# Fused top-k attention and two gated MLPs on one core: where the sign word of the float64 weights is made

## The chip, the cores and the metric

The kernel runs as one program on one core of one Trainium2 chip. The core has five engines with instruction queues of their own that run in order: TensorE (PE in the rows; PEld is its weight load), VectorE (DVE), ScalarE (ACT), GpSimd (POOL) and SyncE (SP), which here only issues DMAs. The metric is the device time of one execution in microseconds (us), lower is better; the median of several executions is compared.

## The reference

q, k and v are float32, 4 batches x 8 heads x 576 tokens x 64. The weights of the two MLPs are not cast: they arrive as float64 in their raw bytes, so the kernel has to turn pairs of 32-bit words into float32 by itself.

```python
scores = scale * np.matmul(q, k.transpose(0, 1, 3, 2))
kth = np.partition(scores, -32, axis=-1)[..., -32:-31]
scores = np.where(scores >= kth, scores, -1e9)
attn = np.exp(scores - np.max(scores, axis=-1, keepdims=True))
attn = attn / (np.sum(attn, axis=-1, keepdims=True) + 1e-09)
x = np.matmul(attn, v)            # to 2304 tokens x 512
g = x @ w_gate                    # 512 x 1536
x = (g / (1 + np.exp(-g)) * (x @ w_val)) @ w_out
h = x @ w_in                      # 512 x 2048
out = (h * np.cos(h)) @ w_out2
```

## The kernel before

**Stages.** The 18 tiles of 128 tokens are cut into ten chunks, two of one tile and eight of two. Each chunk runs through attention for 4 pairs of heads; a unit is one tile and one head, 144 in all. For a unit TensorE makes the scores (L609), ScalarE copies them out (L614), VectorE finds the 32 largest by four rounds of MAX8 (L637) with three MATCH_REPLACE8 between (L640), GpSimd makes two bounds from them (L651, L655), ScalarE makes the exponentials (L668, L679), TensorE transposes them (L701), ScalarE empties PSUM (L706), TensorE multiplies with v (L739, L742). The first MLP follows chunk by chunk behind attention: plain matmuls for the first two chunks (L977, L1043), and for the other eight matmuls with weights and activations split into two float32r parts (L888, L1100). The second MLP (L1313, L1377) comes when all chunks are done and takes the last third of the time.

**Conversion.** One piece of weights is 128 x 512 float64, that is two interleaved int32 planes, the high word `h` and the low word `l`. `convert` issues, for each piece: `cv_high` and `cv_low` on ScalarE (L213, L216), which scale the words in place; one instruction that makes the sign word `y`; `cv_join` on VectorE (L227, called the join below), which shifts `h` and ORs the sign into it; and `cv_add` on GpSimd (L230), an integer add of both words. There are 68 pieces. In 48 of them (24 of the first MLP's gate and value weights, 24 of the second MLP's weights, converted early during attention) the sign is made by `cv_sign` on GpSimd (L224) into an SBUF tile `c0` or `c1`. In the other 20 (12 of the first MLP's output weights, 8 of the second MLP's) it is made by `cv_minus` on ScalarE (L220) into a PSUM tile `y` or `cy`. The 24 pieces of the first MLP use the tiles `c0` and `c1` in turn, so a sign of one piece can be written only when the join two pieces earlier has read its tile; the 24 early pieces of the second MLP use `c1` for the sign and `c0` for the sum.

**Order.** Nothing is scheduled at run time. A planner (`Plan`) runs over all these steps when the program is built: each step yields an engine, a cost in us, a due time and its readiness, and the planner emits, for each engine, the ready step with the earliest due time. Its costs are only numbers in the code; they set the order in which the instructions stand in the engines' queues. On the chip each queue then runs in that order, and an instruction whose input is not there holds up everything behind it on its engine. So a change of a cost, or of a step's engine, rearranges all five queues a little.

Of the kernel before, what the change touches and what calls it, by code (L numbers as in the profile page):

```python
# [9 lines left out]
F32 = mybir.dt.float32  # L10
F32R = mybir.dt.float32r
I32 = mybir.dt.int32
# [3 lines left out]
OP = mybir.AluOpType  # L16
# [6 lines left out]
DM = H * D  # L23
# [133 lines left out]
def topk_attention_moe_moe(ctx: ExitStack, tc: tile.TileContext, qT, kT, vP, w1, wo1, w2, out):  # L157
    nc = tc.nc
# [17 lines left out]
    pools = {}  # L176
# [31 lines left out]
    def due_unit(u):  # L208
        return u * PACE


    def cv_high(h):
        nc.scalar.activation(h.bitcast(F32), h.bitcast(F32), AF.Copy, scale=2.0 ** -112)  # L213

    def cv_low(l):
        nc.scalar.activation(l.bitcast(U32), l.bitcast(U32), AF.Copy, scale=2.0 ** -29)  # L216

    def cv_minus(h, y):

        nc.scalar.activation(y, h.bitcast(F32), AF.Prelu, bias=0.0, scale=2.0 ** 40, alpha=2.0 ** 127)  # L220

    def cv_sign(h, y):

        nc.gpsimd.tensor_scalar(y, h.bitcast(F32), 0.0, -2.0 ** 31, op0=OP.is_lt, op1=OP.mult)  # L224

    def cv_join(h, y):
        nc.vector.scalar_tensor_tensor(h, h, 3, y, op0=OP.logical_shift_left, op1=OP.bitwise_or)  # L227

    def cv_add(h, l, x):
        nc.gpsimd.tensor_tensor(x, h, l, op=OP.add)  # L230

    r_pre, r_wo, r_sign, r_cy2 = Ring(6), Ring(2), Ring(1), Ring(1)
    r_c = [Ring(1) for _ in range(2)]
# [3 lines left out]
    def words(raw):  # L237
        w = raw.rearrange("p (n t) -> p n t", t=2)
        return w[:, :, 1], w[:, :, 0]

    def conv_tile(i):
        return pools["conv"].tile([128, DM], I32, tag=f"c{i}", name=f"c{i}")

    def convert(raw, due, gates, sign, on_act=False, into=None):

        h, l = words(raw)
        yield "ACT", 0.54, lambda: cv_high(h), due, True
        yield "ACT", 0.54, lambda: cv_low(l), due, False
        for gate in gates:
            yield gate  # L250
        st = {}

        def minus():
            st["y"] = sign()
            (cv_minus if on_act else cv_sign)(h, st["y"])

        yield "ACT" if on_act else "POOL", 0.54 if on_act else 0.72, minus, due, not on_act
        joined = yield "DVE", 0.63, lambda: cv_join(h, st["y"]), due, True
        t = yield "POOL", 1.25, lambda: cv_add(h, l, into() if into else l), due, True
        return joined, t  # L260

    W1X, W1, WO = {}, {}, {}
# [6 lines left out]
    def slot(i):  # L269
        return f"w{i - 1}" if i else "wx"  # L270
# [43 lines left out]
    def wo_turn(c, f):  # L314
        return ev_wol.setdefault(c * NF1 + f, Event())
# [5 lines left out]
    def wo_index(c, f):  # L321
        return c * NF1 + f
# [4 lines left out]
    def wo0_free(f, t):  # L327
        r_c[f % 2].free(W1_C + f // 2, t, plan)

    def wo0_proc(f):  # L330

        due = WO_FIRST + WO_STEP * f
        yield r_wo.gate(f)
        st = {}
        if f:
            yield wo_turn(0, f - 1)

        def load():
            st["raw"] = moe.tile([128, DM], I64, tag="wo", name="wo", bufs=r_wo.n)
            nc.sync.dma_start(st["raw"], wo1[f])  # L340

        t = yield "DMA", 2.1, load, due - 6.0, True
        wo_turn(0, f).set(t - plan.LAT["DMA"], plan)
        yield r_c[f % 2].gate(W1_C + f // 2)

        def into():
            WO[f] = conv_tile(f % 2)
            return WO[f]

        joined, t = yield from convert(st["raw"].bitcast(I32), due, [r_sign.gate(f)], lambda: yt[1].bitcast(I32),  # L350
                                       True, into)
        r_sign.free(f, joined, plan)
        r_wo.free(f, t, plan)
        WO[f] = WO[f].bitcast(F32)
        ev_wo[0, f].set(t, plan)
        t = yield "DMA", 1.1, lambda: nc.sync.dma_start(wo32[f], WO[f]), due, True
        wo_whole[f].set(t, plan)
        wo0_free(f, t)
# [6 lines left out]
    def w2_early_proc(i):  # L365
        f, half = divmod(i, 2)
        due = due_unit(46 + 3.8 * i)
        yield ev_w1s[2 * NF1 - 1]
        yield r_raw.gate(i)
        k = W1_C + WO_C + i  # L370
        cs = slice(half * DM, half * DM + DM)
        st = {}

        def load():
            st["raw"] = wpool.tile([128, DM], I64, tag=f"w{2 * NF1 - 1}", name="w2_raw")
            nc.sync.dma_start(st["raw"], w2[f, :, cs])

        yield "DMA", 2.1, load, due - 8.0, True
        yield r_c[0].gate(k)

        def into():
            st["x"] = conv_tile(0)
            return st["x"]

        joined, t = yield from convert(st["raw"].bitcast(I32), due, [r_c[1].gate(k)], lambda: conv_tile(1), False, into)
        r_c[1].free(k, joined, plan)
        r_raw.free(i, t, plan)
        t = yield "DMA", 1.1, lambda: nc.sync.dma_start(w2d[f, :, cs], st["x"].bitcast(F32)), due, True
        r_c[0].free(k, t, plan)
        w2_stored[f].set(t, plan)  # L390
# [801 lines left out]
    def w2_proc(i):  # L1192
        f, half = divmod(i, 2)
        due = T2 - 60.0 + 2.0 * i
        yield ev_pb
        st = {}
        if f < NS2:
            yield w2_stored[f]
            yield r_cvx2.gate(i)

            def load():
                st["x"] = pools["pbc"].tile([128, 512], I32, tag="cvx", name="cvx", bufs=r_cvx2.n)
                nc.sync.dma_start(st["x"].bitcast(F32), w2d[f, :, half * 512:half * 512 + 512])

            yield "DMA", 1.05, load, due, True
        else:
            pc = pools["pbc"]
            n = i - 2 * NS2
            yield r_raw2.gate(n)

            def load():
                st["raw"] = pc.tile([128, DM], I64, tag="w2s", name="w2s", bufs=r_raw2.n)
                nc.sync.dma_start(st["raw"], w2[f, :, half * DM:half * DM + DM])

            yield "DMA", 2.1, load, due, True
            yield r_cvx2.gate(i)

            def into():
                st["x"] = pc.tile([128, DM], I32, tag="cvx", name="cvx", bufs=r_cvx2.n)
                return st["x"]  # L1220

            joined, t = yield from convert(
                st["raw"].bitcast(I32), due, [r_cy2.gate(n)],
                lambda: pools["psB"].tile([128, DM], I32, tag="cy", name="cy", bufs=r_cy2.n), True, into)
            r_cy2.free(n, joined, plan)
            r_raw2.free(n, t, plan)
        if f < NF1:
            yield ev_gemm[NCH - 1, f]
        elif f < NB:
            yield ev_pbx  # L1230
        else:
            yield r_wo.gate(wo_index(NCH, half))
        x = st["x"].bitcast(F32)

        def hi():
            if f < NF1:
                pool, tag, bufs = wpool, slot(i), 1
            elif i == 2 * NB - 1:
                pool, tag, bufs = wpool, f"w{2 * NF1 - 1}", 1
            elif f < NB:  # L1240
                pool, tag, bufs = pools["pbx"], f"w{f}{half}", 1
            else:
                pool, tag, bufs = moe, "wo", r_wo.n
            st["w"] = W2[f, half] = pool.tile([128, 2, DM], F32R, tag=tag, name=f"w2_{f}", bufs=bufs)
            nc.scalar.activation(st["w"][:, 0], x, AF.Copy)  # L1245

        yield "ACT", 0.52, hi, due, True
        eng, name, cost = (nc.vector, "DVE", 0.75) if i % 3 == 2 else (nc.gpsimd, "POOL", 1.25)
        t = yield name, cost, lambda: eng.tensor_sub(st["w"][:, 1], x, st["w"][:, 0]), due, True  # L1249
        r_cvx2.free(i, t, plan)  # L1250
        ev_w2[f].set(t, plan)
# [158 lines left out]
    for f in range(NF1):  # L1410
        plan.start(wo0_proc(f))
    for i in range(2 * NS2):
        plan.start(w2_early_proc(i))
# [21 lines left out]
    for i in range(2 * NF2):  # L1435
        plan.start(w2_proc(i))
# [46 lines left out]
```

## Time and profile before

| what | value |
|---|---|
| median of 3 runs | 1317.35 us (1317.04 to 1320.25) |
| the profiled execution, its own time | 1314.26 us |
| its span, first to last instruction | 1312.5 us |
| mean granted TensorE clock | 0.975 of full |
| busy: PE, DVE | 1206.4 us, 1019.3 us |
| busy: ACT, POOL | 941.3 us, 723.6 us |

Times within the span are counted from its first instruction. Busy time of an engine is the time in which one of its instructions ran. "Idle before" and "waits" name the instruction that waited, and after the arrow what ended its wait last. In a row, `w_raw` is a piece of raw weights, `c` a sign tile, `wo` a piece of output weights with its sign in `y`, `sc` and `s` scores, `b` the bounds, `e` the exponentials, `tp` and `pt` their transposes.

### The profile page before, as it was taken

To read this page: it belongs to the slowest core of one execution; us is meant where nothing else is said; L and a number is where in the kernel's file an instruction comes from. 1 tells how busy PE (TensorE), PEld (TensorE's weight loads), DVE (VectorE), ACT (ScalarE), POOL (GpSimd) and SP (SyncE) were. 2 spreads that over 40 slices of the span, in tenths; PEclk is the share of its full clock that TensorE was granted. 3 is DMA by queue.
4 is the path that set the end of the run, shared out by engine and by line. 5 is a ranking of instruction groups with operands and counts; after the bars stand their busy time and mean duration, and the time that the engine had idled before them with its cause. 6 is when DMAs were issued, how large, how long until landed. Compare 5 with 4: busy or idle time off the path is not lost. (4 is left out here: it accounts for less than half of the span.)

```text
span 1312.5 us, 24509 instructions
## 1 busy us (share of the span) xinstructions
PE 1206.4 (92%) x8544; PEld 1096.7 (84%) x8544; DVE 1019.3 (78%) x2024; ACT 941.3 (72%) x2116; POOL 723.6 (55%) x1087
## 2 busy tenths in 40 slices
PE   2557897899999999999999999998999999999998
PEld 2346575799998899999999999997999999999997
DVE  5888999999999999999999998146655555555554
ACT  5666899888888888888788887447654555555554
POOL 6998578898878887887777765555210000000000
PEclk9768899999999999999999999998999999999999
DMA  6452445455555555546454532584110100000000
GB/s 209 136 189 85 140 158 155 149 158 190 176 160 176 174 173 160 176 147 194 146 164 141 169 115 82 175 283 163 35 43 7 35 14 24 26 8 30 1 25 24
DMA packets 83100, 157.97 MB, mean 120 GB/s; under 512 B 16672, under 2 KB 35104, under 8 KB 82976
## 3 DMA queue, kind: packets, MB, share of 16 engines
q1 hardware_dynamic: 82976, 156.41, 37.6%
q8 instruction: 67, 1.10, 0.3%
q14 instruction: 57, 0.47, 0.1%
HBM read 131.20 MB, written 25.17 MB: 119 GB/s over the span
## 5 line engine op out<-in xcount | busy, mean ns | idle before, releaser
L637 DVE MAX8 m<-w 128x8 f32<-128x576 f32 x432 | 310.4, 744 | 0.8
L888 PE MATMUL gv<-xh,w 128*128 128x256 f32 x1344 | 286.9, 292 | 3.3 <-ACT hg L856 3.3
L888 PEld LDWEIGHTS gv<-xh,w 128*128 128x128 f32 x1344 | 224.4, 190 | 8.4 <-ACT hg L856 4.5
L1313 PE MATMUL h<-x2h,w 128*128 128x384 f32 x768 | 214.1, 340 | 5.5 <-DVE g L1347 5.5
L640 DVE MATCH_REPLACE8 w<-m,w 128x576 f32<-128x576 f32 x288 | 212.7, 740 | 0.0
L1377 PE MATMUL o<-w,gh 128*128 128x512 f32 x576 | 196.4, 396 | 0.0
L888 PE MATMUL gv<-xl,w 128*128 128x256 f32 x672 | 189.7, 282 | 0.0
L1280 POOL TENSOR_TENSOR x2l<-x,x2h 128x384 fp32r<-128x384 f32 x24 | 25.5, 1061 | 252.2 <-ACT x2h L1269 252.2
L1100 PE MATMUL y<-gh,wo 128*128 128x256 f32 x768 | 158.8, 288 | 0.3 <-DMA wo<-wo 0.3
L609 PE MATMUL sc<-K,q 128*128 128x288 f32 (+1 forms) x640 | 127.2, 327 | 30.5 <-DVE K L478 11.4
L1313 PEld LDWEIGHTS h<-x2h,w 128*128 128x128 f32 x768 | 141.6, 189 | 10.5 <-DVE g L1347 6.5
L701 PE MATMUL tp<-ident,e 128*128 128x128 f32 x648 | 113.9, 287 | 33.1 <-ACT pt L706 27.3
L1347 DVE TENSOR_TENSOR g<-r,h 128x384 f32<-128x384 f32 x96 | 53.1, 554 | 115.4 <-ACT r L1342 115.4
L706 ACT ACTIVATE pt<-tp 128x512 f32<-128x512 f32 (+1 forms) x216 | 106.8, 494 | 34.2 <-PE tp L701 32.3
L1313 PE MATMUL h<-x2l,w 128*128 128x384 f32 x384 | 130.1, 339 | 0.0
L1100 PEld LDWEIGHTS y<-gh,wo 128*128 128x128 f32 x768 | 126.2, 190 | 4.3 <-issue 3.6
L609 PEld LDWEIGHTS sc<-K,q 128*128 128x128 f32 (+1 forms) x640 | 98.3, 199 | 37.3 <-DVE K L478 8.8
L888 PEld LDWEIGHTS gv<-xl,w 128*128 128x128 f32 x672 | 128.0, 190 | 0.0
L1340 ACT ACTIVATE r<-r 128x384 f32<-128x384 f32 x96 | 50.3, 525 | 108.3 <-DVE r L1337 108.3
L1377 PEld LDWEIGHTS o<-w,gh 128*128 128x128 f32 x576 | 108.7, 189 | 21.2
L668 ACT ACTIVATE e<-s,b 128x576 f32<-128x576 f32 x144 | 112.9, 784 | 14.2 <-POOL b L651 13.8
L701 PEld LDWEIGHTS tp<-ident,e 128*128 128x128 f32 x648 | 80.7, 146 | 49.9 <-ACT pt L706 38.4
(122 smaller groups left out, 2998.5 us busy)
## 6 DMA issues: line engine op xcount, KB each, us to landing
wo<-wo SPq DMA_DIRECT2D x96, 512.0 KB, 3.7
w_raw<-in_w SPq DMA_DIRECT2D x48, 512.0 KB, 5.1
V<-in_vP SPq DMA_DIRECT2D x52, 256.0 KB, 3.1
kx<-in_kT SPq DMA_DIRECT2D x64, 144.0 KB, 3.0
qx<-in_qT SPq DMA_DIRECT2D x64, 128.0 KB, 3.0
wo<-in_wo SPq DMA_DIRECT2D x12, 512.0 KB, 3.8
wo<-wo SPq DMA_DIRECT2D x24, 256.0 KB, 2.9
w2d<-c SPq DMA_DIRECT2D x24, 256.0 KB, 2.8
```

Of the source, the lines that this page charges most:

```text
L609: nc.tensor.matmul(sc[:r1, s, :HALF], q[:, a, t * 128:t * 128 + r1], k[:, s * HALF:s * HALF + HALF], start=a == 0, stop=a == 1)
L637: nc.vector.max(out=st["m"][:, 8 * i:8 * i + 8], in_=st["w"] if i else st["s"])
L640: nc.vector.match_replace(out=st["w"], in_to_replace=st["m"][:, 8 * i:8 * i + 8], in_values=st["w"] if i else st["s"], imm_value=LOWEST)
L668: nc.scalar.activation(st["e"], st["s"], AF.Prelu, bias=st["b"][:, 1:2], scale=SCALE, alpha=STEEP)
L701: nc.tensor.transpose(st["ps"][:, j - j0], e[:, j * 128:j * 128 + 128], ident)
L706: lambda: nc.scalar.activation(ptT[c, p, t][:, j0:j1], st["ps"][:, :j1 - j0], AF.Copy),
L888: nc.tensor.matmul(gv[g], W1[f, kk // 2][:, a, g, kk % 2], m[:, kk], start=kk == 0 and i == 0, stop=kk == KT - 1 and i == 2)
L1100: nc.tensor.matmul(y1p[d // 2][:, d % 2], w[:, a, d * 128:d * 128 + 128], m, start=f == 0 and i == 0 and d % 2 == 0, stop=f == NF1 - 1 and ...
L1313: nc.tensor.matmul(st["h"], w[:, a, kk * 128:kk * 128 + 128], m[:, kk], start=kk == 0 and n == 0, stop=kk == KT - 1 and n == 2)
L1340: yield "ACT", 0.41, lambda: nc.scalar.activation(r, r, AF.Abs), due, True
L1347: nc.vector.tensor_mul(st["g"], r, h)
L1377: nc.tensor.matmul(o[t], a[:, cs], W2[f, 1][:, m], start=f == 0 and n == 0, stop=f == NF2 - 1 and n == 2)
```

## The change

`cv_sign` is removed, and all 68 pieces make their sign by `cv_minus`, a leaky ramp on ScalarE: positive inputs are scaled by 2^40, negative ones by 2^40 x 2^127, and the conversion to int32 on output saturates at the lowest integer, which is the sign word. For the 48 pieces it writes the same SBUF tiles `c0` and `c1` as before. In the planner the step is charged 0.54 us to ScalarE instead of 0.72 us to GpSimd and stands directly behind `cv_low`, and the add on GpSimd is charged 1.04 us instead of 1.25.

```diff
--- before.py
+++ after.py
@@ -219,10 +219,6 @@
 
         nc.scalar.activation(y, h.bitcast(F32), AF.Prelu, bias=0.0, scale=2.0 ** 40, alpha=2.0 ** 127)
 
-    def cv_sign(h, y):
-
-        nc.gpsimd.tensor_scalar(y, h.bitcast(F32), 0.0, -2.0 ** 31, op0=OP.is_lt, op1=OP.mult)
-
     def cv_join(h, y):
         nc.vector.scalar_tensor_tensor(h, h, 3, y, op0=OP.logical_shift_left, op1=OP.bitwise_or)
 
@@ -241,7 +237,7 @@
     def conv_tile(i):
         return pools["conv"].tile([128, DM], I32, tag=f"c{i}", name=f"c{i}")
 
-    def convert(raw, due, gates, sign, on_act=False, into=None):
+    def convert(raw, due, gates, sign, into=None):
 
         h, l = words(raw)
         yield "ACT", 0.54, lambda: cv_high(h), due, True
@@ -252,11 +248,11 @@
 
         def minus():
             st["y"] = sign()
-            (cv_minus if on_act else cv_sign)(h, st["y"])
-
-        yield "ACT" if on_act else "POOL", 0.54 if on_act else 0.72, minus, due, not on_act
+            cv_minus(h, st["y"])
+
+        yield "ACT", 0.54, minus, due, False
         joined = yield "DVE", 0.63, lambda: cv_join(h, st["y"]), due, True
-        t = yield "POOL", 1.25, lambda: cv_add(h, l, into() if into else l), due, True
+        t = yield "POOL", 1.04, lambda: cv_add(h, l, into() if into else l), due, True
         return joined, t
 
     W1X, W1, WO = {}, {}, {}
@@ -348,7 +344,7 @@
             return WO[f]
 
         joined, t = yield from convert(st["raw"].bitcast(I32), due, [r_sign.gate(f)], lambda: yt[1].bitcast(I32),
-                                       True, into)
+                                       into)
         r_sign.free(f, joined, plan)
         r_wo.free(f, t, plan)
         WO[f] = WO[f].bitcast(F32)
@@ -382,7 +378,7 @@
             st["x"] = conv_tile(0)
             return st["x"]
 
-        joined, t = yield from convert(st["raw"].bitcast(I32), due, [r_c[1].gate(k)], lambda: conv_tile(1), False, into)
+        joined, t = yield from convert(st["raw"].bitcast(I32), due, [r_c[1].gate(k)], lambda: conv_tile(1), into)
         r_c[1].free(k, joined, plan)
         r_raw.free(i, t, plan)
         t = yield "DMA", 1.1, lambda: nc.sync.dma_start(w2d[f, :, cs], st["x"].bitcast(F32)), due, True
@@ -1221,7 +1217,7 @@
 
             joined, t = yield from convert(
                 st["raw"].bitcast(I32), due, [r_cy2.gate(n)],
-                lambda: pools["psB"].tile([128, DM], I32, tag="cy", name="cy", bufs=r_cy2.n), True, into)
+                lambda: pools["psB"].tile([128, DM], I32, tag="cy", name="cy", bufs=r_cy2.n), into)
             r_cy2.free(n, joined, plan)
             r_raw2.free(n, t, plan)
         if f < NF1:
```

The line numbers of the changed kernel are 4 lower from `cv_join` on (L223 is the join, L226 the add). The rows below are from the instruction queues of the two programs; the letters behind an underscore are buffer numbers.

VectorE, around the first joins, before:

```order
L637 MAX m<-w 128x8 x2
L640 MATCH_REPLACE w<-m,w 128x576
L637 MAX m<-s 128x8
L637 MAX m<-w 128x8
L227 SCALAR_TENSOR_TENSOR w_raw<-w_raw,c_229 128x512
L227 SCALAR_TENSOR_TENSOR w_raw<-w_raw,c_239 128x512
L640 MATCH_REPLACE w<-m,s 128x576
```

and the same place in the changed kernel:

```order
L633 MAX m<-w 128x8 x2
L636 MATCH_REPLACE w<-m,w 128x576
L223 SCALAR_TENSOR_TENSOR w_raw<-w_raw,c_221 128x512
L633 MAX m<-w 128x8
L223 SCALAR_TENSOR_TENSOR w_raw<-w_raw,c_237 128x512
L633 MAX m<-s 128x8 x2
L636 MATCH_REPLACE w<-m,s 128x576
```

The joins stand two instructions or one earlier among the searches and no longer back to back.

ScalarE at the same time, before (L213 and L216 are the two passes over `h` and `l`):

```order
L213 ACTIVATE w_raw<-w_raw 128x512
L473 ACTIVATE K<-kx 128x576
L216 ACTIVATE w_raw<-w_raw 128x512
L213 ACTIVATE w_raw<-w_raw 128x512
L216 ACTIVATE w_raw<-w_raw 128x512
L213 ACTIVATE w_raw<-w_raw 128x512
L216 ACTIVATE w_raw<-w_raw 128x512
L668 ACTIVATE e<-s,b_236 128x576
```

and in the changed kernel:

```order
L213 ACTIVATE w_raw<-w_raw 128x512
L469 ACTIVATE K<-kx 128x576
L216 ACTIVATE w_raw<-w_raw 128x512
L220 ACTIVATE c_221<-w_raw 128x512
L213 ACTIVATE w_raw<-w_raw 128x512
L216 ACTIVATE w_raw<-w_raw 128x512
L220 ACTIVATE c_237<-w_raw 128x512
L664 ACTIVATE e<-s,b_230 128x576
L213 ACTIVATE w_raw<-w_raw 128x512
L216 ACTIVATE w_raw<-w_raw 128x512
L523 ACTIVATE q<-qx 128x128
L220 ACTIVATE c_259<-w_raw 128x512
```

The sign instruction (L220) follows the two passes of its piece, and the third piece is begun after the first exponential and not ahead of it.

GpSimd at the same time, before:

```order
L478 TENSOR_TENSOR K<-kx,K 64x576
L224 TENSOR_SCALAR c_229<-w_raw 128x512
L651 TENSOR_TENSOR b_236<-m,cst 128x2
L224 TENSOR_SCALAR c_239<-w_raw 128x512
L655 TENSOR_TENSOR b_236<-b_236 128x1
L651 TENSOR_TENSOR b_244<-m,cst 128x2
L655 TENSOR_TENSOR b_244<-b_244 128x1
L230 TENSOR_TENSOR w_raw<-w_raw 128x512 x2
```

and in the changed kernel:

```order
L474 TENSOR_TENSOR K<-kx,K 64x576
L647 TENSOR_TENSOR b_230<-m,cst 128x2
L651 TENSOR_TENSOR b_230<-b_230 128x1
L226 TENSOR_TENSOR w_raw<-w_raw 128x512
L647 TENSOR_TENSOR b_245<-m,cst 128x2
L226 TENSOR_TENSOR w_raw<-w_raw 128x512
L651 TENSOR_TENSOR b_245<-b_245 128x1
```

The two sign instructions (L224) that stood ahead of and between the small instructions of the bounds `b` are gone from this queue.

## Rows read from the trace of the kernel before

**Rows 1.** Busy time of each engine by stretch (us); (x) counts instructions

```profile
core 0: us, PE busy (x) PEld busy (x) DVE busy (x) ACT busy (x) POOL busy (x), PEclk, DMA share, GB/s
...
15.00:110.00 95.00, 49.94 (x241) 38.53 (x242) 78.95 (x152) 66.07 (x143) 88.96 (x95) 0.80 0.53 173
...
160.00:200.00 40.00, 37.82 (x222) 29.07 (x220) 39.90 (x82) 39.47 (x90) 31.91 (x52) 1.00 0.47 154
200.00:250.00 50.00, 40.33 (x247) 28.01 (x246) 50.00 (x110) 44.38 (x100) 40.46 (x56) 0.93 0.46 134
250.00:800.00 550.00, 537.75 (x4827) 513.82 (x4826) 534.91 (x1110) 459.89 (x1112) 437.68 (x727) 1.00 0.52 163
...
905.00:1312.00 407.00, 401.61 (x1992) 362.11 (x1992) 218.16 (x387) 226.17 (x439) 31.96 (x28) 0.99 0.08 26
```

**Rows 2.** Waits from 15 to 110 us: us in total, times, longest

```profile
DVE w_raw L227 <- POOL c L224: 15.9, 16, 2.3
...
ACT e L668 <- POOL b L651: 12.9, 8, 3.5
ACT s L614 <- PE sc L609: 5.4, 5, 2.9
ACT rs L787 <- PE tp L781: 5.3, 4, 1.9
...
PE tp L701 <- ACT pt L706: 16.4, 7, 5.0
```

**Rows 3.** GpSimd groups by line, 15 to 110 us: busy us, mean ns, idle before

```profile
L224 POOL TENSOR_SCALAR c<-w_raw 128x512 int32<-128x512 f32 x21 | 42.9, 2045 | 0.1
L230 POOL TENSOR_TENSOR w_raw<-w_raw 128x512 int32<-128x512 int32 x21 | 22.1, 1059 | 2.4 <-DVE w_raw L227 1.4 <-ACT e L679 0.9
```

**Rows 4.** The join on VectorE by line, 15 to 110 us

```profile
L227 DVE SCALAR_TENSOR_TENSOR w_raw<-w_raw,c 128x512 int32<-128x512 int32 x21 | 19.2, 912 | 16.1 <-POOL c L224 15.9
```

**Rows 5.** The join in the whole span, by tile: ns least, median, most

```profile
L227 DVE SCALAR_TENSOR_TENSOR w_raw<-w_raw,c x48: 668/694/1798, 23.8 to 762.4; 128x512 int32<-128x512 int32 x48
L227 DVE SCALAR_TENSOR_TENSOR wo<-wo,y x12: 662/672/697, 135.2 to 198.0; 128x512 int32<-128x512 int32 x12
```

**Rows 6.** The ramp of line 220 on ScalarE, and who waited for it

```profile
L220 ACT ACTIVATE y<-wo x12: 609/651/755, 126.7 to 196.6; 128x512 int32<-128x512 f32 x12
...
  DVE wo L227: 1.3, 1
```

**Rows 7.** Timeline of ScalarE, two conversion passes and the next instruction

```profile
40.70 0.66 ACT L213 ACTIVATE w_raw<-w_raw 128x512 f32<-128x512 f32 x1
41.26 0.65 ACT L216 ACTIVATE w_raw<-w_raw 128x512 uint32<-128x512 uint32 x1
41.81 0.29 ACT L554 ACTIVATE q<-qx 128x128 fp32r<-128x128 f32 x1
```

**Rows 8.** Timeline, an integer add and a join that start together

```profile
34.47 1.04 POOL L230 TENSOR_TENSOR w_raw<-w_raw 128x512 int32<-128x512 int32 x1
34.54 1.52 DVE L227 SCALAR_TENSOR_TENSOR w_raw<-w_raw,c 128x512 int32<-128x512 int32 x1 [1.20 <-POOL c L224]
```

**Rows 9.** Waits from 260 to 800 us

```profile
DVE w_raw L227 <- POOL c L224: 3.0, 2, 2.4
...
PE tp L701 <- ACT pt L706: 3.4, 10, 0.7
...
PE gv L888 <- ACT hg L856: 2.7, 4, 1.1
```

**Rows 10.** The split matmuls of line 888: ns, first and last start

```profile
L888 PE MATMUL gv<-xh,w x1344: 274/283/388, 246.3 to 838.3; 128*128 128x256 f32 x192
```

**Rows 11.** Chain that ended last from 905 us on, by line

```profile
by line: PE h L1313 49.1%; PE o L1377 48.9%; DVE g L1347 0.3%; ACT r L1340 0.2%; ACT w L1245 0.2%; ACT ot L1395 0.1%; ACT w2s L216 0.1%; ACT w2s L213 0.1%; issue 0.1%; ACT r L1342 0.1%; ACT cy L220 0.1%; ACT k L1327 0.0%
```

**Rows 12.** Waits of the whole span

```profile
DVE w_raw L227 <- POOL c L224: 20.7, 20, 2.4
```

## The prediction, made before the changed kernel ran

> **What bounds the kernel now.** I read the end first. In the chain that ended last, from 905 us on, 98% is matmuls of the second MLP (49.1% L1313, 48.9% L1377), and TensorE is busy 401.6 of 407 us there [rows 11, 1]. The change puts nothing into that third, so it can only move the moment at which it begins. From 250 to 800 us two engines are full side by side: TensorE 537.8 and VectorE 534.9 of 550 us, the clock granted in full [rows 1]. ScalarE has 459.9 (84%) there, GpSimd 437.7 (80%). TensorE's work in this part is the same before and after; its steady part begins with the first split matmul at 246.3 us [rows 10]. Ahead of that, from 160 to 250 us, VectorE is busy 89.9 of 90 us [rows 1], and the searches it makes there feed the chunk that the split matmuls wait for. So whatever VectorE gains before 160 us is handed on: the first split matmul comes that much earlier, and with it the end, as long as neither engine loses it again in the 550 us behind.
>
> The opening is different. From 15 to 110 us (95 us) GpSimd is busy 89.0 us, VectorE 79.0, ScalarE 66.1, TensorE 49.9 [rows 1]. GpSimd is the bound. The waits say the same: VectorE's joins waited 15.9 us in 16 cases for the sign, and that is nearly all of its 16.0 us of idle time; ScalarE's exponentials waited 12.9 us for the bounds, which stand behind signs in GpSimd's queue; TensorE's transposes wait on ScalarE for 16.4 us in turn [rows 2]. In the whole span joins waited 20.7 us for signs, so three quarters of it lies here [rows 12].
>
> **What is removed.** 48 signs on GpSimd. In the opening they are 21, 42.9 us of its 89.0, 2.05 us each [rows 3]. Without them GpSimd has 46.1 us of work left in this stretch and bounds nothing.
>
> **What is added.** 48 ramps on ScalarE. The 12 ramps of the trace take 651 ns in the median [rows 6], but consecutive passes over the same shape start 0.55 to 0.56 us apart [rows 7], so one costs its queue 0.56 us. In the opening that is 21 x 0.56 = 11.8 us, and ScalarE would have 77.9 us of work.
>
> The page "ScalarE: Activation LUTs" of the Trainium skill (Rules for kernel authors) speaks against this move: it lists the ramp among the functions for VectorE and not for ScalarE, and counts about 0.3 us an instruction with 0.83 ns an element. For 512 elements that is an estimate of 0.72 us, 15.2 us in the opening and 81.3 us of work for ScalarE; by it the floor below would lie some 3 us higher. The rows' 0.56 us decides, and VectorE, with 79.0 us of its own, is the wrong place for more work here.
>
> **The opening's sum, from both sides.** On VectorE's side: the 12 joins whose sign ScalarE makes today waited 1.3 us for it in all, 0.11 us each [rows 6]. If the 21 joins wait like that, 2.3 us of the 15.9 come back: a gain of 13.6 us. The joins themselves may shorten. They take 912 ns in the mean here [rows 4], against 694 in the median of all 48 and 672 for the 12 that read their sign from PSUM [rows 5]. Some of the long ones begin in the moment in which GpSimd, done with the sign, begins its next add: 1.52 us at 34.54 [rows 8]. That coincidence goes, since GpSimd no longer releases the join; chance overlaps with adds remain. 21 x (912 - 694) = 4.6 us is the most, so VectorE's side allows 13.6 to 18.2 us.
>
> On ScalarE's side: how full can it get? From 160 to 200 us it is busy 39.5 of 40 us while VectorE is too [rows 1], so it can run at 98.7%; 77.9 us of work then need 79 us, and the stretch could shrink by 16 us. But in the opening it also waits on TensorE, 5.4 us for scores and 5.3 for row sums [rows 2]; if those stay whole, 77.9 + 10.7 = 88.6 us, and only 6.4 us are gained. Those waits are partly echoes of late bounds, but not all. Between 6.4 and 16 I take the middle, **11 us**: below VectorE's lower figure, because ScalarE's queue will be the fullest one in this stretch.
>
> **The rest.** From 250 to 800 us the 24 early pieces of the second MLP each put 0.56 us more on ScalarE, 13.4 us on an engine with 90 us to spare [rows 1]. The price if the cover fails: the sign stands directly behind two other passes, 1.7 us in one piece, and what is queued behind it are the instructions that empty PSUM for TensorE. TensorE waits on those little today, 3.4 us for transposes and 2.7 for gates [rows 9]. On the other side the joins' 3.0 us of waits for signs go there [rows 9], and GpSimd loses 24 x 2.05 = 49 us of work that bounds nothing. I set the sum of this at a loss of 1 us, with 0 to 13.4 as bounds for the loss. The planner's other edit, 1.25 to 1.04 us for the add, costs nothing on the chip (adds take 1.06 us [rows 3]); it and the moved step rearrange the queues, which I count as noise of some 3 us either way. DMA is as before; its share in the opening, 0.53 [rows 1], would rise to about 0.60 when the same bytes move in 84 us.
>
> **Sum.** -11 + 1 = -10 us. Against the profiled execution (1314.26 us, 1312.5 of them the span) that is 1304.3; the median of the runs shown lies 3.1 us higher, so I forecast **1307 us** there.
>
> **Rivals.**
> - *VectorE gets all of it.* Waits go, and the joins too: 15.9 + 4.6 = 20.5 us, with nothing lost behind: 1297. The page "SBUF — State Buffer" of the Trainium skill (section Who interferes with whom) gives the mechanism: a VectorE instruction with two SBUF inputs and a GpSimd instruction that reads SBUF exclude each other for a whole instruction. The trace agrees: joins with both inputs in SBUF reach 1798 ns, those with the sign in PSUM never exceed 697 [rows 5]. For this: GpSimd's load falls by half. Against: the adds stay, and ScalarE is nearly full. Chance 0.12.
> - *The wait only changes its name.* The sign on ScalarE waits for its tile until the join two pieces earlier is done, and holds up scores and exponentials behind it. If each of the 21 costs VectorE what it costs today, 15.9 / 21 = 0.76 us, only the joins' shortening is left, about 2 us: 1315. For this: the two tiles are shared in turn, and ScalarE is in order. Against: the 0.11 us of the joins that ScalarE serves today. Chance 0.18.
> - *Slower: ScalarE becomes the bound.* All 48 ramps land on the path, in the opening through the exponentials and later through the emptying of PSUM: 48 x 0.56 = 26.9 us, less the 20.7 us of waits removed, gives +6: 1324. It decides when more than 20.7 / 48 = 0.43 us of each ramp's 0.56 is exposed. For this: ScalarE at 84% for 550 us beside two full engines. Against: TensorE's few waits on it. Chance 0.09.
> - That the change does not do what it says is excluded by the queues: 48 instructions leave GpSimd's and 48 join ScalarE's.
>
> **Chances and range.** The forecast's own mechanism, a gain of 6 to 15 us (1302 to 1311), has 0.60; 0.01 is for what I have not thought of. What can be told from no change here is about 0.3%, 4 us, so faster means below 1313.4: 0.60 + 0.12 and a part of the second rival, 0.76. Same 0.15, slower 0.09. The range for 8 in 10 runs from the bigger gain to just past the wait that only changes its name: 1298 to 1317.
>
> **What the profile would show.** Right: from 15 us on, what was reached at 110 us is reached near 99; GpSimd's share of the opening falls from 94% to some 55%, ScalarE's rises above 90%; the joins' waits fall from 15.9 us to 2 to 4; the first split matmul starts near 235 instead of 246.3; the second MLP begins 10 us earlier and lasts as long as before. Wrong: the first split matmul moves as said, but the second MLP does not, then ScalarE took it back between 250 and 800, and TensorE's waits on L702 and L852 have grown; or joins wait for L220 as they did for L224; or the joins stay at 912 ns and VectorE's busy time with them.

## The result, and the profile of the changed kernel

The changed kernel takes 1285.0 us in the median (1283.9 to 1286.1, 4 runs) against 1317.2 (1316.9 to 1320.3, 4 runs): a ratio of 0.975, 95% interval 0.9733 to 0.9768. That is 32 us faster, three times the gain that was forecast, and below the range. The profiled execution took 1285.8 us, its span 1284.0; against the span of before, 1312.5, that is 28.5 us (the execution profiled before was itself 3 us under its median).

Where the 28.5 us came from is read from one row, line 884's first and last start (line 888 before, [rows 10]):

```profile
L884 PE MATMUL gv<-xh,w x1344: 274/283/388, 222.3 to 811.4; 128*128 128x256 f32 x192
```

The first split matmul starts 24.0 us earlier (246.3 to 222.3). From the first to the last it is 589.1 us where it was 592.0, a gain of 2.9. From the last to the end of the span it is 472.6 where it was 474.2, a gain of 1.6. So five sixths of the gain are made ahead of the first split matmul.

Busy time by stretch in the changed kernel, columns as in [rows 1]:

```profile
core 0: us, PE busy (x) PEld busy (x) DVE busy (x) ACT busy (x) POOL busy (x), PEclk, DMA share, GB/s
...
15.00:110.00 95.00, 63.24 (x320) 50.72 (x320) 91.33 (x190) 87.70 (x191) 54.93 (x92) 1.00 0.55 184
110.00:160.00 50.00, 44.58 (x258) 32.53 (x257) 49.34 (x105) 48.00 (x112) 30.25 (x60) 0.97 0.51 158
...
250.00:800.00 550.00, 539.07 (x4858) 517.77 (x4859) 528.78 (x1099) 470.32 (x1134) 386.26 (x701) 1.00 0.51 159
876.00:1284.00 408.00, 399.98 (x1992) 359.12 (x1992) 218.51 (x389) 227.78 (x443) 31.81 (x29) 1.00 0.09 28
```

In the opening GpSimd is no longer full (54.9 of 95 us), and VectorE (91.3) and ScalarE (87.7) both nearly are. The last 408 us are what the last 407 were.

Its waits from 15 to 110 us (us in total, times, longest), to be read beside [rows 2]:

```profile
POOL w_raw L226 <- DVE w_raw L223: 17.2, 15, 1.9
...
PE sc L605 <- ACT s L610: 13.0, 8, 2.6
...
PE tp L697 <- ACT pt L702: 8.2, 4, 3.3
...
ACT rx L791 <- PE av L738: 5.0, 4, 1.4
...
DVE w_raw L223 <- ACT c L220: 3.7, 6, 1.0
...
ACT s L610 <- PE sc L605: 1.2, 2, 0.9
```

The join's wait has gone from 15.9 us to 3.7, the exponentials' wait for the bounds (12.9) is gone from the list, and a wait of 17 us now stands before GpSimd's add, on an engine with 40 us to spare. ScalarE's own waits on TensorE, 5.4 us for scores and 5.3 for row sums before, are 1.2 us for scores and none for row sums; but 5.0 us now stand before L791, which takes the product with v (`av`) out of PSUM. So some 6 of the 11 us are still there, under another name.

All 24 pieces of the first MLP's weights now pass within the opening. The join from 15 to 130 us, which holds all 24 in both kernels, in the kernel before and then in the changed one (busy us, mean ns, idle before):

```profile
L227 DVE SCALAR_TENSOR_TENSOR w_raw<-w_raw,c 128x512 int32<-128x512 int32 x24 | 21.6, 899 | 17.9 <-POOL c L224 17.8
```

```profile
L223 DVE SCALAR_TENSOR_TENSOR w_raw<-w_raw,c 128x512 int32<-128x512 int32 x24 | 16.9, 705 | 3.7 <-ACT c L220 3.7
```

So VectorE got back 17.8 - 3.7 = 14.1 us of waits and 21.6 - 16.9 = 4.7 us in the joins themselves, 18.8 us. What it made of them is seen in the number of searches (MAX8) that it has started by a moment: a unit needs four, with three replacements between. The searches alone, from the start to two moments, before and after:

```profile
core 0: us, DVE busy (x), PEclk, DMA share, GB/s
...
0.00:126.50 126.50, 42.19 (x59) 0.82 0.49 158
0.00:200.00 200.00, 79.32 (x112) 0.87 0.48 154
```

```profile
core 0: us, DVE busy (x), PEclk, DMA share, GB/s
...
0.00:126.50 126.50, 53.23 (x75) 1.00 0.54 174
0.00:200.00 200.00, 90.92 (x128) 0.97 0.53 168
```

At 126.5 us the changed kernel is 16 searches ahead, and at 200 us still 16. With 0.745 us for a search and 0.74 for each of three replacements to four searches, one search stands for some 1.3 us, so the lead is about 21 us: the 18.8 us, within two searches. It is made wholly while the joins run and kept from then on.

### The profile page after: what moved, and what is told of

It reads as the page before. It is cut to its first block, busy times and chain, and to the rows that moved or that the text cites. A ratio compares the mean times of both kernels' runs of the same rounds, so it can differ in the third digit from the quotient of the medians.

```text
span 1284.0 us, 24500 instructions
## 1 busy us (share of the span) xinstructions
PE 1199.9 (93%) x8544; PEld 1092.0 (85%) x8544; DVE 1014.5 (79%) x2024; ACT 963.7 (75%) x2164; POOL 626.6 (49%) x1039
## 4 chain that ended last, share of the span: by engine, by line
PE 64%; DVE 12%; ACT 11%; DMA 5%; POOL 3%; issue 3%; SPq 1%; POOLq 0%; ACTq 0%; DVEq 0%
PE o L1373 15%; PE h L1309 15%; PE gv L884 11%; PE y L1096 8%; DVE m L633 6%; DVE w L636 5%; PE av L738 4%; PE sc L605 3%; PE tp L697 3%; PE gv L973 3%; DMA wo<-wo 1%; ACT pt L702 1%; PE gvl L884 1%; DMA y<-yo 1%; ACT s L610 1%
## 5 line engine op out<-in xcount | busy, mean ns | idle before, releaser
L605 PE MATMUL sc<-K,q 128*128 128x288 f32 (+1 forms) x640 | 126.6, 327 | 34.0 <-ACT s L610 14.6
L697 PE MATMUL tp<-ident,e 128*128 128x128 f32 x648 | 111.8, 283 | 21.8 <-ACT pt L702 18.1
L675 ACT ACTIVATE e<-e,b 128x576 f32<-128x576 f32 x144 | 112.9, 784 | 3.2 <-POOL b L651 1.4
L633 DVE MAX8 m<-s 128x8 f32<-128x576 f32 x144 | 107.3, 746 | 9.4 <-ACT s L610 6.2
```

The costliest lines, as they stand in the source:

```text
L605: nc.tensor.matmul(sc[:r1, s, :HALF], q[:, a, t * 128:t * 128 + r1], k[:, s * HALF:s * HALF + HALF], start=a == 0, stop=a == 1)
L633: nc.vector.max(out=st["m"][:, 8 * i:8 * i + 8], in_=st["w"] if i else st["s"])
L675: nc.scalar.activation(st["e"], st["e"], AF.Exp, bias=st["b"][:, 2:3], scale=1.0, accum_out=smT[c, p][:, j:j + 1])
L697: nc.tensor.transpose(st["ps"][:, j - j0], e[:, j * 128:j * 128 + 128], ident)
```

## The experiments

A table first, with the working behind it below. "Opening" is the first start of a split matmul, "middle" the time from there to the last one, both from the row of line 888 (884, 886 or 894 where the lines moved). The median of before lay between 1317.2 and 1319.3 us on the chips used.

| kernel | median us | ratio to before (95%) | opening | middle |
|---|---|---|---|---|
| before | 1317.2 | | 246.3 | 592.0 |
| changed | 1285.0 | 0.975 (0.9733 to 0.9768) | 222.3 | 589.1 |
| e9: old order, ramp | 1294.8 | 0.9831 (0.9814 to 0.9848) | 228.3 | 589.3 |
| e10: new order, comparison | 1316.4 | 0.9987 (0.9974 to 1.0001) | 243.4 | 595.9 |
| e3: before, add charged 1.04 | 1309.2 | 0.9924 (0.9885 to 0.9963) | 236.7 | 598.4 |
| e13: before, add charged 1.10 | 1306.2 | 0.9914 (0.9898 to 0.9931) | 240.0 | 593.1 |
| e14: before, add charged 0.98 | 1306.8 | 0.9915 (0.9889 to 0.9942) | 244.1 | 591.0 |
| e7: changed, add charged 1.25 | 1292.3 | 0.9811 (0.9789 to 0.9833) | 223.4 | 588.3 |
| e15: changed, add charged 1.10 | 1276.7 | 0.9693 (0.9679 to 0.9708) | 225.8 | 580.1 |
| e16: changed, add charged 0.98 | 1283.8 | 0.9753 (0.9723 to 0.9782) | 225.1 | 585.6 |
| e4: before, sign charged 2.0, add 1.04 | 1297.0 | 0.9829 (0.98 to 0.9858) | 234.5 | 589.2 |
| e5: changed, 24 idle comparisons on GpSimd | 1301.1 | 0.9875 (0.9856 to 0.9894) | 236.9 | 583.4 |
| e6: changed, 24 ramps twice | 1296.1 | 0.9835 (0.9813 to 0.9857) | 240.2 | 586.6 |
| e1: ramp for the first 24 alone | 1282.9 | 0.9722 (0.969 to 0.9753) | 224.5 | 588.1 |
| e2: ramp for the later 24 alone | 1296.8 | 0.9827 (0.9795 to 0.9859) | 238.1 | 590.3 |
| e8: e1, later signs charged 2.0 | 1274.6 | 0.9674 (0.9658 to 0.9691) | 222.7 | 581.9 |
| e11: e8, every second early sign on GpSimd | 1281.8 | 0.972 (0.9679 to 0.9761) | 226.5 | 583.7 |
| e12: e8, every third | 1281.8 | 0.9721 (0.9685 to 0.9757) | 226.1 | 584.3 |

### Engine or order

The change does two things at once: the sign runs elsewhere, and the planner, told of it, writes another order. Two kernels part them. **e9** keeps the old plan to the last row and only issues the ramp where the plan put the comparison:

```diff
-            (cv_minus if on_act else cv_sign)(h, st["y"])
+            cv_minus(h, st["y"])
```

> The plan of the kernel before, to the instruction: VectorE's and TensorE's queues are the same as before, row by row. Only at the places where the 48 signs were emitted, the ramp goes to ScalarE's queue in place of the comparison to GpSimd's. So the engine changes and the order does not. If the engine is what counts: most of the gain, 1285 to 1295, joins' waits for the sign under 5 us. If the order that follows from truer costs is what counts: 1305 to 1315.

Measured: 1294.8 us, 23 us under before. The opening in that kernel, then the join's wait and ScalarE's two waits on TensorE in it, and the 24 joins from 15 to 130 us:

```profile
15.00:110.00 95.00, 60.78 (x311) 47.96 (x311) 89.65 (x183) 87.92 (x191) 55.49 (x91) 0.89 0.56 184
```

```profile
DVE w_raw L227 <- ACT c L220: 5.3, 9, 1.1
...
ACT rs L787 <- PE tp L781: 3.8, 4, 1.5
...
ACT s L614 <- PE sc L609: 2.2, 4, 0.9
```

```profile
L227 DVE SCALAR_TENSOR_TENSOR w_raw<-w_raw,c 128x512 int32<-128x512 int32 x24 | 18.1, 760 | 5.3 <-ACT c L220 5.3
```

The joins' wait is just above the 5 us that were expected, the time within its range. The first split matmul starts 18.0 us earlier than before, the middle is 2.7 shorter. This is the gain of the engine alone. **e10** is the counterpart: the plan of the changed kernel, charged to ScalarE, with the comparison issued on GpSimd for the 48 pieces.

```diff
-            cv_minus(h, st["y"])
+            (cv_sign if pool else cv_minus)(h, st["y"])
```

> The mirror: the plan of the changed kernel, but at the 48 places the sign is issued as GpSimd's comparison. The order is the new one, the engine the old one; the plan now charges GpSimd nothing for 2.0 us of work. If the engine counts: the gain is gone or worse, 1312 to 1330, joins' waits for the sign over 15 us. If the order counts: 1285 to 1300.

Measured: 1316.4 us, nothing gained. The opening, and the join's wait:

```profile
15.00:110.00 95.00, 47.93 (x220) 37.51 (x222) 79.05 (x157) 62.39 (x136) 83.94 (x95) 1.00 0.50 167
```

```profile
DVE w_raw L227 <- POOL c L224: 15.8, 17, 1.3
```

15.8 us of waits, as before. So the new order by itself is worth nothing (it was made for a sign that takes no time on GpSimd), the engine by itself 23 us, and the new order on top of the ramp the other 10 (1294.8 to 1285.0). e10 also settles a side question. The granted clock of TensorE in the opening was 0.80 before and 1.00 in the changed kernel; in e10 it is 1.00 and the first split matmul comes only 2.9 us earlier than before, so the higher clock does not make the gain.

### What a cost in the planner is worth

**e3** takes the other edit of the change, the add's charge, into the kernel before; **e13** and **e14** try values beside it. **e7**, **e15** and **e16** do the same with the changed kernel.

```diff
-        t = yield "POOL", 1.25, lambda: cv_add(h, l, into() if into else l), due, True
+        t = yield "POOL", 1.04, lambda: cv_add(h, l, into() if into else l), due, True
```

> The kernel before with only the planner's cost of the integer add changed from 1.25 to 1.04 us, so nothing but the order in the queues differs. Theory A: noise of the order, 1314 to 1320 us. Theory C (a part of the gain is a better order by truer costs): faster by more than 4 us, below 1313.

> The kernel before with the add charged 1.10 us in the planner (1.25 before; 1.04 gave 1309 and measured adds take 1.06). If the 9 us are owed to a truer cost: 1306 to 1311 again. If each small change of a cost draws another order by chance: anywhere from 1300 to 1325, with no trend in the cost.

> The kernel before with the add charged 0.98 us. Truer cost: about as 1.04, 1306 to 1311. Chance: anywhere from 1300 to 1325.

> The changed kernel with only the planner's cost of the integer add put back from 1.04 to 1.25 us; no instruction changes its engine. If the order is noise by now: within 5 us of the changed kernel, 1280 to 1290. If the truer cost carried a part of the gain here as it did alone (9 us): 1291 to 1297.

> The changed kernel with the add charged 1.10 us instead of 1.04 (1285.0; 1.25 gave 1292). Truer cost: 1284 to 1287. Chance: anywhere from 1275 to 1295.

> The changed kernel with the add charged 0.98 us. Truer cost: 1284 to 1287. Chance: anywhere from 1275 to 1295.

Measured on the kernel before: -9 us with 1.04, -11 with 1.10, -10 with 0.98. Measured on the changed kernel: 1.25 gives 1292.3, the three values near the measured 1.06 us of an add ([rows 3]) give 1276.7, 1285.0 and 1283.8. Two things follow. In both kernels all three charges near the truth are faster than 1.25, by 9 to 11 and by 7 to 16 us. Only one charge far from the truth was tried, so that truth makes the gain, and not a poor order that 1.25 happens to draw, is likely and not shown. And among charges that are all near the truth the times scatter over 8 us in the changed kernel, with disjoint ranges of single runs (1276.2 to 1277.3 with 1.10, 1283.9 to 1286.1 with 1.04), though no instruction differs, only the order. 1276.7 lies outside what "truer cost" expected and inside "chance". So the change's own 1285.0 is one draw from such a spread.

**e4** charges the sign what it costs, and leaves it on GpSimd:

```diff
-        yield "ACT" if on_act else "POOL", 0.54 if on_act else 0.72, minus, due, not on_act
+        yield "ACT" if on_act else "POOL", 0.54 if on_act else 2.0, minus, due, not on_act
...
-        t = yield "POOL", 1.25, lambda: cv_add(h, l, into() if into else l), due, True
+        t = yield "POOL", 1.04, lambda: cv_add(h, l, into() if into else l), due, True
```

> The kernel before with the sign on GpSimd, but charged its measured 2.0 us in the planner (0.72 before) and the add 1.04. Theory A (GpSimd is loaded to 94% in the opening, and no order takes that away): 1312 to 1318 us, GpSimd still busy over 90% from 15 to 110 us. Theory C (the waits come from a plan that thought the sign three times too short, so the joins stood too early in VectorE's queue): most of the opening's 24 us come back, 1293 to 1300, with the joins' waits for the sign below 5 us.

Measured: 1297.0 us, 21 us under before, and 12 under e3, which has the same charge for the add. The opening:

```profile
15.00:110.00 95.00, 58.86 (x279) 44.35 (x279) 94.99 (x190) 71.03 (x152) 87.99 (x99) 0.96 0.57 184
```

Three of its waits in that stretch, the last of them VectorE's only one, and then VectorE's longest from 180 to 270 us:

```profile
ACT s L614 <- PE sc L609: 7.1, 5, 2.1
...
ACT rs L787 <- PE tp L781: 3.3, 3, 1.8
...
DVE m L637 <- ACT s L614: 0.5, 1, 0.5
```

```profile
DVE m L637 <- ACT s L614: 8.1, 4, 4.0
```

GpSimd is as full as before (88.0 us), and yet VectorE is busy for 95.0 of 95 us: a plan that knows the sign takes 2 us puts the join behind more searches, and no join waits. The joins stay long (the first 24 take 883 ns in the mean, 705 in the changed kernel), but VectorE has begun 64 searches by 110 us, where it had begun 50 before and 63 in the changed kernel. So the 15.9 us of [rows 2] were not the price of a full GpSimd alone. They were the price of joins that stood in VectorE's queue where a sign of 0.72 us would have been ready. Of that lead 8 us are lost again behind 180 us, 6 of them ahead of the first split matmul, where searches wait for scores.

### What GpSimd's and ScalarE's time is worth

**e5** adds to the changed kernel 24 comparisons of the old form on GpSimd, on a tile of their own that nobody reads; **e6** runs the first 24 ramps twice.

```diff
+        yield ("POOL", 0.72, lambda: nc.gpsimd.tensor_scalar(x.bitcast(I32), x, 0.0, -2.0 ** 31, op0=OP.is_lt,
+                                                             op1=OP.mult), due, True)
```

```diff
         yield "ACT", 0.54, minus, due, False
+        if extra:
+            yield "ACT", 0.54, lambda: cv_minus(h, st["y"]), due, False
```

> The changed kernel with 24 dead instructions of the old sign's form on GpSimd in the opening, on a tile of their own that nobody reads, placed where the first MLP's signs used to be and charged 0.72 us as those were; nothing waits for them but GpSimd's queue. Theory A1 (what costs is GpSimd's time: bounds and adds late, joins stretched by chance overlaps): 24 x 2.0 = 48 us of load again, at least half of the opening's gain is lost, 1297 us or more. Theory A2 (what cost was VectorE's join waiting for a sign made late): under a quarter is lost, 1285 to 1291.

> The changed kernel with the ramp of the 24 first pieces run twice on ScalarE, into the same tile: 24 x 0.56 = 13.4 us more on its queue in the opening. If ScalarE is the bound there as the prediction's ceiling had it: 8 to 14 us slower than the changed kernel, 1293 to 1299. If it still has slack: 0 to 4 us slower, 1285 to 1289.

Measured: e5 1301.1 us, 16 over the changed kernel (the execution profiled was the fastest of four, 1296.3). The opening, and two waits in it:

```profile
15.00:110.00 95.00, 56.64 (x265) 43.73 (x266) 85.80 (x176) 79.93 (x173) 91.75 (x104) 1.00 0.56 183
```

```profile
DVE w_raw L223 <- ACT c L220: 8.1, 7, 3.2
...
ACT e L685 <- POOL b L661: 3.0, 2, 2.1
```

No join waits for these comparisons, and half of the 32 us is lost all the same. GpSimd is full again and exponentials wait for bounds again; the ramps stand behind them in ScalarE's queue, and the join now waits 8.1 us for a ramp instead of 3.7. So GpSimd's time does count, under a plan that charges it too low. The 24 comparisons were charged 0.72 us, so the order is another one too, and its part was not taken out.

e6 takes 1296.1 us, 11 more than the changed kernel for 24 x 0.56 = 13.4 us of added ramps:

```profile
15.00:110.00 95.00, 51.87 (x253) 41.30 (x254) 88.00 (x177) 87.82 (x183) 47.35 (x82) 0.77 0.55 182
```

ScalarE is busy 87.8 us, as in the changed kernel, with fewer instructions of its own work done. By the time alone about 0.46 of each added ramp's 0.56 us comes out at the end, as expected of a ScalarE without slack. But the first split matmul comes 17.9 us later, more than the 13.4 us that were added, and all that follows it is 6.5 us shorter. The plan was charged for the second ramps and wrote another order, and the clock granted in the opening is 0.77. So this run fits a full ScalarE and does not isolate the price of a ramp.

### First 24 and later 24

**e1** moves only the first MLP's 24 signs, **e2** only the 24 later ones; both charge the add 1.04.

```diff
-        yield "ACT", 0.54, minus, due, False
+        yield "POOL" if pool else "ACT", 0.72 if pool else 0.54, minus, due, pool
```

> Only the 24 pieces of the first MLP make their sign on ScalarE; the 24 early pieces of the second MLP go back to GpSimd. Theory A (all of the gain is made in the opening, in GpSimd's queue): as the changed kernel, 1285 us, within 4 us, first split matmul near 222 us. Theory B (the relief of GpSimd or the shorter joins between 250 and 800 us count too): 2 to 5 us more, 1287 to 1290. By the prediction's own third term (24 ramps cost ScalarE's queue 1 us): 1284.

> The other half: only the 24 early pieces of the second MLP make their sign on ScalarE, the first MLP's stay on GpSimd. Theory A: no gain, 1314 to 1320 us, first split matmul near 246 us. Theory B: 2 to 5 us faster than before, 1312 to 1315.

Measured: e1 1282.9 us, e2 1296.8; with e3 (neither, 1309.2) and the changed kernel (both, 1285.0) that makes a square. The later 24 alone gain 12 us, the first 24 alone 26, both together 24. e1 and the changed kernel can't be told apart (their ranges of single runs, 1280.2 to 1285.1 and 1283.9 to 1286.1, overlap), so with the first 24 moved the later 24 are worth nothing; with the first 24 left in place the later ones take 8.1 us off the middle (598.4 to 590.3) and 3.8 off what lies behind it. e2 fits neither of its expectations. The terms don't add. **e8** is e1 with the later signs charged 2.0 us instead of 0.72:

```diff
-        yield "POOL" if pool else "ACT", 0.72 if pool else 0.54, minus, due, pool
+        yield "POOL" if pool else "ACT", 2.0 if pool else 0.54, minus, due, pool
```

> As the run with only the first 24 signs on ScalarE, and the 24 later signs on GpSimd charged their measured 2.0 us instead of 0.72. Later signs make VectorE wait hardly at all, so by the theory of the opening: no change against that run, 1279 to 1287. By the theory that wrong costs cost time wherever they stand: 3 to 6 us faster, 1277 to 1280.

Measured: 1274.6 us, ratio 0.9674, the fastest of all and 10 us under the changed kernel, with this row of split matmuls:

```profile
L888 PE MATMUL gv<-xh,w x1344: 274/283/388, 222.7 to 804.6; 128*128 128x256 f32 x192
```

That is below both expectations. The opening is that of the changed kernel; the middle is 581.9 us instead of 589.1, and from the last split matmul to the end it is 468.6 instead of 472.6. But e15, with all signs on ScalarE, has a middle of 580.1 and comes within about 2 us of e8 by its order alone. So the 10 us can be had by order; that they come from leaving the later signs on GpSimd is not shown.

**e11** and **e12** give every second, or every third, of the first 24 back to GpSimd, charged 2.0 us.

```diff
-        joined, t = yield from convert(raw, due, [ring.gate(n)], lambda: conv_tile(i % 2))
+        joined, t = yield from convert(raw, due, [ring.gate(n)], lambda: conv_tile(i % 2), None, i % 2 == 1)
```

> As the run with the first 24 signs on ScalarE and the later 24 on GpSimd at 2.0 us (1274.6 us), but of the first 24 every second goes back to GpSimd too, charged 2.0 us. It gives ScalarE 12 x 0.56 = 6.7 us back in the opening, where it is busy 92%, and GpSimd 24 us more on 59%. If ScalarE's fullness in the opening still costs: 2 to 6 us faster, 1269 to 1273. If the joins' waits for GpSimd come back: 4 to 12 us slower, 1279 to 1287.

> The same with every third of the first 24 pieces on GpSimd (8 of 24). Between the two: if ScalarE's fullness costs, 1270 to 1273; if the joins' waits come back, 1278 to 1284.

Measured: 1281.8 us for both, 7 us slower than e8 (on another chip; 6 us between the profiled executions). The times are those expected if the joins' waits came back, but joins wait under 2 us in both openings. VectorE is busy 93.5 and 93.6 of 95 us, more than in e8 (91.1), and not with more work: by 110 us it has begun 62 and 63 searches, in e8 62, and its first 24 joins take 790 and 804 ns in the mean instead of 708. At 200 us all three have begun 128, yet the first split matmul comes 3.8 and 3.4 us later and the middle is about 2 us longer. Giving ScalarE room by sharing the signs did not help. What those 7 us wait for was not found.

## Why the prediction was wrong

**What bounds the kernel now: right in the place, half right in the cause.** The gain is made in the opening, handed on through VectorE's full stretch, and the second MLP is untouched. The lead of 16 searches at 126.5 us and at 200 us shows the handing on. "GpSimd is the bound" was half of it: e4 has a GpSimd as full and no join that waits, and e10 has the new order and all the waits. A full GpSimd made the wait under a plan that charged its sign 0.72 us (or, in e10, nothing) where it takes 2.05. Whether the wrong charge would make it with GpSimd idle in part was not tested; in the middle, with GpSimd 80% busy, the same charge cost the joins 3.0 us ([rows 9]).

**The opening's sum: the step that failed.** "Between 6.4 and 16 I take the middle, 11 us: below VectorE's lower figure, because ScalarE's queue will be the fullest one" was too small; with the order held (e9) the first split matmul comes 18.0 us earlier. e9 has the queues of before, row by row, so each engine's lead can be read at any point. The 161st instruction of VectorE is reached at 110 us before and at 95.4 in e9, a lead of 14.6 us; the 237th at 150 us and at 131.1, a lead of 18.9. In the kernel before and then in e9:

```profile
0.00:110.00 110.00, 83.62 (x161) 0.83 0.54 173
0.00:150.00 150.00, 119.78 (x237) 0.84 0.46 150
```

```profile
0.00:95.40 95.40, 79.99 (x161) 0.89 0.62 201
0.00:131.10 131.10, 115.64 (x237) 0.91 0.53 171
```

And two neighbours in ScalarE's queue, before and then in e9:

```profile
114.47 0.58 ACT L706 ACTIVATE pt<-tp 128x512 f32<-128x512 f32 x1
120.97 0.38 ACT L993 ACTIVATE th<-gv 128x256 f32<-128x256 f32 x1 [5.92 <-POOL vv L1003]
```

```profile
102.62 0.60 ACT L706 ACTIVATE pt<-tp 128x512 f32<-128x512 f32 x1
103.09 0.39 ACT L993 ACTIVATE th<-gv 128x256 f32<-128x256 f32 x1
```

So two things were wrong in the step, and neither was the size of its bounds.

- The cap. ScalarE's own lead is 12 us at 110 us and still 11.9 at L706, about the 11 of the forecast, and its waits on TensorE do last by more than half (6.0 of 10.7 us in e9). But what is handed on is VectorE's lead, and that is 14.6 us there, within VectorE's own 13.6 to 18.2. A ScalarE that lags behind VectorE costs VectorE only the 5.3 us for which joins wait for ramps, instead of the 2.3 of the forecast.
- The edge. The sum was drawn at 110 us, with 21 of the 24 joins. Behind it the kernel before still loses time that e9 does not: 5.9 us at one place on ScalarE, which waits for a product that stands behind signs in GpSimd's queue, and on VectorE 1.8 us for the last joins' signs, 1.3 for a ramp of the output weights and 0.7 for a row sum. There both leads grow to 18.9 us.

VectorE's terms were sized well. Over the 24 joins e9 gets back 12.5 us of waits (17.8 to 5.3) and 3.5 in the joins themselves (21.6 to 18.1), the changed kernel 14.1 and 4.7, against 13.6 and "4.6 is the most".

**"Noise of some 3 us either way": the second step that failed.** The planner's charge for the add is worth 9 to 11 us on the kernel before (e3, e13, e14), and 7 on the changed one (e7). The charge was wrong by 0.2 us and was set near the truth by the change; the sign's charge was wrong by 1.3 us, and with the ramp that error went too. Both numbers stood in the diff beside the rows that refuted them ([rows 3]), and the prediction read them as costing nothing on the chip, which they do, and not as a possible gain in order. In the sum that is the 10 us between e9 and the changed kernel (7.8 between the two profiled executions).

**The rest: near in size, other in sign.** Behind the first split matmul a loss of 1 us was set; with the order held (e9) the middle is 2.7 us shorter. e1, which does without the 24 later ramps, can't be told from the changed kernel. In the profiled executions the three parts make up the whole miss: the gain was 28.5 us and not 10, by 7.0 in the opening, 3.7 behind it and 7.8 by order.

**The rivals.** "VectorE gets all of it" (1297, chance 0.12) had the right mechanism; e9, which is that rival without the new order, measured 1294.8. The agreement is in part luck: its 20.5 us were to be there at 110 us, where e9 has 14.6, and the rest came behind, 2.7 of it in the middle. The range began at 1298 and left this rival out. The wait did not change its name: joins wait 3.7 us for the ramp. ScalarE did not take more than it gave, though e6 suggests that there is little room for more. The page of the Trainium skill that the prediction cites against the move, "ScalarE: Activation LUTs" (Rules for kernel authors), names `relu` there, the plain ramp, and not the leaky one.

**What the profile was to show.** Joins' waits of 2 to 4 us: 3.7. GpSimd's share some 55%: 54.9 of 95 us, 58%. ScalarE above 90%: 92%. What was reached at 110 us near 99: with the order held 95.4 on VectorE and 98 on ScalarE. The first split matmul near 235: it is 222.3, which is the error once more.

**Open.** The middle takes 580 to 598 us in these kernels, with the same work, and follows the order in ways that no single wait explained; why the first and the later 24 don't add, and the 7 us of e11 and e12, belong to it. Why an order by truer charges was faster in every pair that was tried (the add in both kernels, the sign in e4 and e8) was not traced to single waits outside the opening.

## What to carry to other kernels

Where a planner writes the queues from a table of costs, hold each cost against its duration in the trace before anything else: here a sign charged 0.72 us and taking 2.05 made a wait that charging it truly also removed, with no instruction moved to another engine. To part an edit's effect on the chip from its effect on the order, issue the new instruction under the old plan and the old one under the new plan. And before a full neighbour is taken as a cap, ask which engine's lead is handed on, and for how long that engine waits for the neighbour; count the wait that goes up to the moment at which the waiting engine is full, not to a round number.

## What the runs showed of the hardware

How far a join is stretched by GpSimd. In e5 the comparisons run beside joins that don't depend on them, so that their overlap is by chance. Three pairs on the timeline (start us, duration us):

```profile
64.32 1.98 POOL L245 TENSOR_SCALAR dead<-dead 128x512 int32<-128x512 f32 x1
65.48 0.69 DVE L223 SCALAR_TENSOR_TENSOR w_raw<-w_raw,c 128x512 int32<-128x512 int32 x1 [3.19 <-ACT c L220]
...
96.83 2.01 POOL L245 TENSOR_SCALAR dead<-dead 128x512 int32<-128x512 f32 x1
97.11 0.91 DVE L223 SCALAR_TENSOR_TENSOR w_raw<-w_raw,c 128x512 int32<-128x512 int32 x1
...
101.33 2.00 POOL L245 TENSOR_SCALAR dead<-dead 128x512 int32<-128x512 f32 x1
101.44 1.07 DVE L223 SCALAR_TENSOR_TENSOR w_raw<-w_raw,c 128x512 int32<-128x512 int32 x1
```

A join begun 0.11 us after the comparison takes 1.07 us, one begun 0.28 after it 0.91, and one begun 1.16 after it 0.69, its undisturbed time, though the comparison runs on for 0.82 us more. The stretched two end as if they had stood still until some 0.5 us into the comparison. All runs together have 33 joins that began during a comparison of 1.7 to 2.2 us. The 16 that began 0.06 to 0.43 us after its start all ended 1.18 to 1.22 us after it; the 17 that began 0.60 us or more after it took 0.67 to 0.70 us. Beside an add a join begun 0.07 us later took 1.52 ([rows 8]), as if it had stood still for 0.9 of the add's 1.04 us. The Trainium skill, "SBUF — State Buffer" (SBUF: two separate sides; Who interferes with whom), says that a VectorE instruction with two SBUF inputs contends with a GpSimd instruction that reads SBUF, and calls the contention an exclusive lock, held for the whole instruction. The traces agree that there is one, and show that for the comparison it doesn't last as long as the instruction.
